# Batch 0's q and k in two parts of 256 and 320 tokens, four heads side by side

## The chip, the core and the metric

The kernel runs on one core of a Trainium2 chip. The core has a matrix engine (TensorE, "PE" in the profile, its weight loads "PEld"), a vector engine (VectorE, "DVE"), a scalar engine (ScalarE, "ACT"), GpSimd ("POOL"), which here mainly issues the loads, and SyncE ("SP"), which issues the stores. Each works through its own instructions in order and waits for the others by semaphores. The metric is the device time of one execution in microseconds (us); lower is better.

## What is computed

Eight batches of eight heads with 576 tokens of 64 elements. Heads 0 to 3 attend to the last 32 tokens, heads 4 to 7 to every fourth of the last 128. The attention's result, with the heads of a token side by side (4608 x 512), goes through two layers with a SiLU between them.

```python
scores = scale * np.matmul(q, k.transpose(0, 1, 3, 2))
rel = pos[:, None] - pos[None, :]
mask_plain = (rel >= 0) & (rel < window)                                   # window = 32
mask_dil = (rel >= 0) & (rel < window * dilation) & (rel % dilation == 0)  # dilation = 4
masks = np.stack([mask_plain if h < H // 2 else mask_dil for h in range(H)], axis=0)
scores = np.where(masks[None, :, :, :], scores, -1000000000.0)
attn = softmax over the last axis
x = np.matmul(attn, v), heads of a token side by side                      # 4608 x 512
h = x @ w_in                                                               # 512 x 2048
g = h * (1.0 / (1.0 + np.exp(-h)))
return (g @ w_out).astype(np.float32)                                      # 2048 x 512
```

## The kernel before

A batch goes through attention and then through the two layers. In the steady state the attention of later batches is spread by a hand-written plan (`plan_of`) between the products of the layers of an earlier one, so TensorE has products while the other engines do the softmax. Batch 0 has nothing to hide behind. It is written out by hand at the end of the kernel (lines 846 to 871), and it is cut into two parts of the sequence: part 0 is tokens 0 to 255, part 1 tokens 256 to 575. In the code z = 0 stands for the plain heads 0 to 3 and z = 1 for the dilated heads 4 to 7, `which` is 0 for q and 1 for k.

**Loads.** All loads are issued by GpSimd and change f32 to f16 on the way. Their order (lines 185 to 205) is: k and q of the dilated heads, the identity matrix, k and q of the plain heads (each a whole 576 tokens of four heads, `load_one`, line 108), two selections that build the band of the mask, v in eight loads, w_in in four quarters, batch 1's q and k, w_out in four quarters, batch 1's v. GpSimd uses eight semaphores in turn for them: a load is issued only when the eighth one before it has landed.

**Transposes.** Attention needs q and k with the 64 elements along the partitions. `transpose` (line 247) does that on TensorE, by products with the identity, into two PSUM tiles of pool `ps` (four buffers), and copies each tile to SBUF with one DVE copy and one ACT copy (`both`). The dilated heads land in `kC` and `qC`, sorted into the four classes of a token's number modulo 4; the plain ones in `kT` and `qT`. For batch 0 each of these four transposes takes the whole sequence, in the order k dilated, q dilated, k plain, q plain.

**Scores to values for batch 0.** `scores0(z, part)` (line 379) puts the mask into a PSUM tile of pool `big` (two buffers) by a product, adds the scores, and lets DVE take each row's maximum. `shift0` has DVE subtract it, after which ACT makes one exponential of the whole tile; or `scaled` scales the maximum and ACT makes one exponential for each of 8, 10 or 12 pieces, with its row sum (`exps`, line 499). `total` sums where ACT did not. `turn0` is DVE's normalisation and 32x32 transposition. `values0(z, part, idle)` (line 636) issues `idle` identity products of 256 columns and then the products with v; `finish0` casts the result to `xT`, by ACT for the dilated and DVE for the plain heads.

**Layer one for batch 0.** `layer1_part(f, part)` (line 683) multiplies w_in with part 0 or part 1 of `xT`; its first call issues three identity products more. Part 0 of all 2048 columns comes first, and into it are put `values0` of part 1 of the dilated heads (before the third group of four tiles) and of the plain heads (before the fourth). The SiLU of ACT writes `gT` (line 704), which layer two reads.

The order of each engine's instructions is the order of the calls. That of batch 0 is:

```python
    scores0(0, 0)
    scaled(0, 0)
    exps(0, 0, 0)
    turn0(1, 0)
    scores0(1, 1)
    scaled(1, 1)
    values0(1, 0, 3)
    finish0(1, 0, (act, act))
    exps(0, 1, 1)
    turn0(0, 0)
    scores0(0, 1)
    values0(0, 0, 2)
    finish0(0, 0)
```

Of the kernel before, what the change touches and what calls it, by code (L numbers as in the profile page):

```python
# [8 lines left out]
F16 = mybir.dt.float16  # L9
# [7 lines left out]
P = 128  # L17
W = 32
DIL = 4
# [4 lines left out]
HF = P // 2  # L24
URS = (9, 12)
DT = (3, 2)


@with_exitstack
def kernel(  # L30
# [9 lines left out]
    nc = tc.nc  # L40
# [51 lines left out]
    def tiles_qk(b):  # L92

        for which in (0, 1):
            t = nat.tile([P, GN[0] * QB + GN[1] * GW], F16, tag=f"n{which}", name=f"n{which}_{b}")
            sq = [
                t[:, 0 : GN[0] * QB].rearrange("p (g e) -> p g e", e=QB),
                t[:, GN[0] * QB :].rearrange("p (g e) -> p g e", e=GW),
            ]
            t = t[:, 0 : 2 * sum(URS) * D].rearrange("p (u d) -> p u d", d=D)  # L100
            u0, u1 = 2 * URS[0], 2 * (URS[0] + URS[1])
            qk[b, 0, which] = t[:, 0:u0].rearrange("p (h u) d -> p h u d", h=2)
            qk[b, 1, which] = t[0 : 2 * UPS[1] if b == 0 else P, u0:u1].rearrange("p (h u) d -> p h u d", h=2)
            for z in (0, 1):
                if b >= DT[z]:
                    qk[b, z, which] = sq[z]

    def load_one(b, z, which):

        src = (q, k)[which]  # L110
        if z == 0 or b == 0:
            nc.gpsimd.dma_start(  # L112
                out=qk[b, z, which].rearrange("p h u d -> p h (u d)"),
                in_=src[b, z * HH : z * HH + HH].rearrange("(h i) (p u) d -> (i p) h (u d)", i=2, u=URS[z]),
            )
            return
        for i in (0, 1):
            h = HH + 2 * i
            nc.gpsimd.dma_start(
                out=qk[b, z, which][i * HF : i * HF + UPS[z]].rearrange("p h u d -> p h (u d)"),  # L120
                in_=src[b, h : h + 2].rearrange("h (p u) d -> p h (u d)", u=URS[z]),
            )

    def load_squares(b, z, which):

# [50 lines left out]
    def load_w_out(c):  # L176
# [5 lines left out]

    band = cpool.tile([P, KB], F32, name="band")
    nc.vector.memset(band[0:W], 0.0)
    tiles_qk(0)
    load_one(0, 1, 1)
    load_one(0, 1, 0)
    make_identity(nc, ident)
    load_one(0, 0, 1)
    load_one(0, 0, 0)  # L190
    nc.gpsimd.affine_select(
        out=band[0:W], in_=band[0:W], compare_op=ALU.is_ge, fill=NEG,
        base=-1, pattern=[[1, KB]], channel_multiplier=-1,
# [2 lines left out]
        out=band[0:W], in_=band[0:W], compare_op=ALU.is_ge, fill=NEG,  # L196
        base=W, pattern=[[-1, KB]], channel_multiplier=1,
    )
    load_v(0)
    for c in range(4):  # L200
        load_w_in(c)
# [45 lines left out]
    def transpose(b, z, which, copies):  # L247

        a = att(b)
        src, n, ur = qk[b, z, which], UPS[z], URS[z]
        ts = [ps.tile([P, ur, n], F16, tag="ps", name=f"t{which}_{b}_{z}_{i}") for i in (0, 1)]
        if z and b == 0:
            for h in (0, 1):
                t = ts[h].rearrange("d (e i r) p -> d e i r p", i=2, r=2)
                for u in range(0, ur, 2):
                    nc.tensor.transpose(
                        t[:, u // DIL, :, u % DIL // 2, :],
                        src[:, h, u : u + 2, :].rearrange("p u d -> p (u d)"),  # L260
                        ident[0 : 2 * n, 0 : 2 * n],
                    )
        else:
            for u in range(0, ur, 1 + z):
                for h in (0, 1):
                    for i in (0, 1):
                        r = slice(i * HF, i * HF + n)
                        if z == 0:
                            o = (h + i) % 2 * D
                            dst, w = ts[h][o : o + D, u, :], src[r, h, u, :]  # L270
                        else:
                            dst = ts[i][:, u // DIL * 4 + 2 * h + u % DIL // 2, :]
                            w = src[r, h, u : u + 2, :].rearrange("p u d -> p (u d)")
                        nc.tensor.transpose(dst, w, ident[r, r])
        for i in (0, 1):
            if z == 0:
                o = (a["qT"][:, i], a["kT"][:, i, W:])[which]
                copies[i](o.rearrange("d (p u) -> d p u", u=ur), ts[i].rearrange("d u p -> d p u"))
            else:
                to_classes(a, which, i, ts[i].rearrange("d (e m) p -> d e m p", m=4), copies[i])  # L280

    def flat(b, z, which):

# [45 lines left out]
    def score(b, h, j, dst, start=True):  # L329

        if b >= DT[0]:
            score_turned(b, 0, h, 0, j, dst)
            return
        a = att(b)
        hp = h // 2
        o = (h + hp) % 2 * D
        r = slice(o, o + D)
        nc.tensor.matmul(
            dst[h * QB : h * QB + QB],
            a["qT"][r, hp, j * QB : j * QB + QB],  # L340
            keys(b, a["kT"][r, hp, j * QB : j * QB + KB]),
            start=start,
            stop=True,
            skip_group_check=not start,
        )
# [33 lines left out]
    def scores0(z, part):  # L379
# [20 lines left out]
        if z:  # L400
            for t in range(n):
                for e in (0, 1):
                    for h in range(HH):
                        for m in (0, 1):
                            score_class(0, h, 2 * e + m, 2 * part + t, sd[:, m, e * n + t], False)
        else:
            for j in range(w):
                for h in range(HH):
                    score(0, h, 8 * part + j, sd[:, j], False)
        nm = att(0)["nm", z, part] = stat.tile([P, WM], F32, tag="nm", name=f"nm_0_{z}_{part}")  # L410
        raw = sd[:, :, 0 : 2 * n] if z else sd[:, 0:w]
        d = nm[:, 0:w].rearrange("p (m t) -> p m t", m=2) if z else nm[:, 0:w]
        nc.vector.tensor_reduce(out=d, in_=raw, axis=AX.X, op=ALU.max, negate=True)
        a = att(0)
        a["raw", z, part] = raw

    def shift0(z, part):

# [264 lines left out]
    def layer1_part(f, part):  # L683
# [3 lines left out]
        n, w = ((4, SA), (2, 512))[part]  # L687
        if part == 0 and f == 0:
            hs = [ps.tile([P, 2, w], F32, tag="ps", name=f"h_0_{f}_{part}_{x}") for x in (0, 1)]
            warm(hs[0].rearrange("p n w -> p (n w)"), 3)  # L690
        else:
            hs = [big.tile([P, n, w], F32, tag="big", name=f"h_0_{f}_{part}")]
        m = n // len(hs)
# [148 lines left out]
    def turn0(z, part):  # L842
        normal(0, z, part)
        turned(0, z, part)

    transpose(0, 1, 1, both)
    build_mask_b()
    transpose(0, 1, 0, both)
    scores0(1, 0)
    shift0(1, 0)  # L850
    transpose(0, 0, 1, both)
    exps(0, 1, 0)
    transpose(0, 0, 0, both)
    total(0, 1, 0)
    scores0(0, 0)
    scaled(0, 0)
    exps(0, 0, 0)
    turn0(1, 0)
    scores0(1, 1)
    scaled(1, 1)  # L860
    values0(1, 0, 3)
    finish0(1, 0, (act, act))
    exps(0, 1, 1)
    turn0(0, 0)
    scores0(0, 1)
    values0(0, 0, 2)
    finish0(0, 0)
    shift0(0, 1)
    exps(0, 0, 1)
    turn0(1, 1)  # L870
# [51 lines left out]
```

## Time and profile before

| | |
|---|---|
| median of 3 runs | 307.88 us (306.43 to 309.94) |
| the profiled execution | 306.95 us, its span 305.1 us |
| busy: PE, PEld | 292.7 us (96% of the span), 186.9 us (61%) |
| busy: ACT, DVE, POOL | 206.4 us (68%), 199.7 us (65%), 119.6 us (39%) |
| layer-one products of batches 1 to 7 (L671) | 113.4 us |
| layer-two products of batches 1 to 7 (L740) | 113.8 us |
| DMA, read and written | 40.75 MB and 9.44 MB |

The profile is of one execution, by the hardware profiler; its span is the time from the first to the last instruction of the program, and the rest of the execution's time lies around it. A busy time is the sum of the stretches in which an engine worked at something. TensorE is the busiest engine, but products are pipelined and their ends are modelled, so its busy share is an upper one. A share over the whole span mixes the start, in which batch 0's attention has nothing beside it, with the long stretch after it.

### The profile page before, as it was taken

To read this page: it belongs to the slowest core of one execution; us is meant where nothing else is said; L and a number is where in the kernel's file an instruction comes from. 1 tells how busy PE (TensorE), PEld (TensorE's weight loads), DVE (VectorE), ACT (ScalarE), POOL (GpSimd) and SP (SyncE) were. 2 spreads that over 40 slices of the span, in tenths; PEclk is the share of its full clock that TensorE was granted. 3 is DMA by queue.
4 is the path that set the end of the run, shared out by engine and by line. 5 is a ranking of instruction groups with operands and counts; after the bars stand their busy time and mean duration, and the time that the engine had idled before them with its cause. 6 is when DMAs were issued, how large, how long until landed. Compare 5 with 4: busy or idle time off the path is not lost.

```text
span 305.1 us, 10290 instructions
## 1 busy us (share of the span) xinstructions
PE 292.7 (96%) x4400; PEld 186.9 (61%) x4400; DVE 199.7 (65%) x354; ACT 206.4 (68%) x688; POOL 119.6 (39%) x182
## 2 busy tenths in 40 slices
PE   2889999999999999999999999999999999999995
PEld 2458654577545774477645775477644775477544
DVE  2886589538898868966895768966895762820012
ACT  2497687865999559965894559975795559546200
POOL 8745347979964295336806086250000000000000
PEclk9999999999999999999999999999999999999999
DMA  6999999999994899499949199390002001110021
GB/s 109 158 205 206 208 157 170 189 185 126 118 184 87 89 70 128 119 106 41 126 71 184 37 62 134 106 118 4 3 34 105 37 2 36 54 52 0 19 86 69
DMA packets 111805, 30.47 MB, mean 100 GB/s; under 512 B 95520, under 2 KB 107280, under 8 KB 111760
## 3 DMA queue, kind: packets, MB, share of 16 engines
q0 software_dynamic: 106432, 20.38, 80.7%
q1 hardware_dynamic: 5328, 9.44, 8.5%
q8 instruction: 34, 0.56, 0.7%
q14 instruction: 11, 0.09, 0.1%
HBM read 40.75 MB, written 9.44 MB: 164 GB/s over the span
## 4 chain that ended last, share of the span: by engine, by line
PE 69%; DMA 16%; POOL 5%; DVE 4%; ACT 3%; issue 2%; POOLq 0%
PE h L671 32%; PE o L740 31%; DMA w_out<-in_moe_w_out_dram 5%; DMA n<-in_q_dram 5%; DMA w_in<-in_moe_w_in_dram 4%; PE x L588 3%; ACT pe L519 2%; DMA n<-in_k_dram 2%; PE s L327 2%; POOL n L132 2%; POOL n L112 1%; DMA vw<-in_v_dram 1%; DVE pn L541 1%; POOL w_in L171 1%; DVE ob L725 1%
## 5 line engine op out<-in xcount | busy, mean ns | idle before, releaser
L679 ACT ACTIVATE gT<-h 128x576 f16<-128x576 f32 x112 | 73.0, 651 | 60.5 <-PE h L671 60.4
L740 PE MATMUL o<-w_out,gT 128*128 128x512 f16 (+1 forms) x528 | 113.8, 373 | 0.0
L671 PE MATMUL h<-xT,w_in 128*128 128x288 f16 x896 | 113.4, 286 | 0.0
L671 PEld LDWEIGHTS <-w_in 128*128 128x128 f16 x896 | 86.6, 98 | 23.5 <-issue 0.2
L740 PEld LDWEIGHTS <-gT 128*128 128x128 f16 x528 | 50.7, 98 | 55.4
L519 ACT ACTIVATE pe<-ms,nm 128x64 f32<-128x64 f32 x238 | 78.9, 333 | 0.1
L725 DVE COPY ob<-o 128x512 f32<-128x512 f32 (+1 forms) x35 | 22.8, 664 | 45.4 <-PE o L740 44.1
L519 ACT ACTIVATION_READ_ACCUMULATOR pe<-ms,nm 128x1 f32 x238 | 44.5, 187 | 0.0
L132 POOL DMA_DIRECT2D n<-in_k_dram x44 | 31.9, 736 | 26.2 <-DVE kC L300 25.1
L372 DVE SCALAR_TENSOR_TENSOR ms<-s,mask 128x512 f32<-128x512 f32 x28 | 19.2, 686 | 28.6 <-PE s L327 19.9
L132 POOL DMA_DIRECT2D n<-in_q_dram x44 | 31.9, 735 | 3.5 <-DMA n<-in_q_dram 3.1
L154 POOL DMA_DIRECT2D vw<-in_v_dram x32 | 18.4, 580 | 34.4 <-PE x L588 31.8
L541 DVE TENSOR_TENSOR pn<-pe,r 128x640 f16<-128x640 f32 (+2 forms) x32 | 25.3, 792 | 1.1
L557 DVE STREAM_TRANSPOSE pt<-pn 128x640 f16<-128x640 f16 (+4 forms) x32 | 24.7, 772 | 1.1
L163 POOL DMA_DIRECT2D vw<-in_v_dram x32 | 21.1, 665 | 9.7 <-DMA w_out<-in_moe_w_out_dram 8.0
L439 DVE TENSOR_REDUCE nm<-ms 128x10 f32<-128x640 f32 (+1 forms) x28 | 22.0, 786 | 1.0
L696 PE MATMUL h<-xT,w_in 128*128 128x256 f16 (+1 forms) x128 | 18.6, 302 | 0.0
L588 PEld LDWEIGHTS <-vw 32*64 32x64 f16 (+1 forms) x1264 | 13.1, 107 | 7.4 <-issue 6.7
L588 PE MATMUL x<-pt,vw 32*64 32x64 f16 (+2 forms) x1264 | 15.0, 193 | 0.9 <-DVE pt L557 0.8
L696 PEld LDWEIGHTS <-w_in 128*128 128x128 f16 x128 | 12.7, 103 | 3.9 <-issue 0.2
L623 DVE CAST xT<-x 128x288 f16<-128x288 f32 x22 | 15.0, 819 | 0.0
L716 PE MATMUL o<-w_out,gT 128*128 128x512 f16 x64 | 14.7, 380 | 0.2 <-ACT ob L725 0.2
(84 smaller groups left out, 209.7 us busy)
## 6 DMA issues: line engine op xcount, KB each, us to landing
out_dram<-ob SPq DMA_DIRECT2D x35, 256.0 KB, 3.0
n<-in_k_dram POOLq DMA_DIRECT2D x24, 108.0 KB, 4.8
n<-in_q_dram POOLq DMA_DIRECT2D x24, 108.0 KB, 5.3
vw<-in_v_dram POOLq DMA_DIRECT2D x31, 80.0 KB, 3.7
vw<-in_v_dram POOLq DMA_DIRECT2D x32, 72.0 KB, 4.0
w_in<-in_moe_w_in_dram POOLq DMA_DIRECT2D x4, 512.0 KB, 9.3
w_out<-in_moe_w_out_dram POOLq DMA_DIRECT2D x4, 512.0 KB, 11.7
n<-in_k_dram POOLq DMA_DIRECT2D x20, 72.0 KB, 3.7
```

The source lines that it names most:

```text
L132: nc.gpsimd.dma_start(out=qk[b, z, which][o : o + QB], in_=bass.AP((q, k)[which].tensor, (b * H + z * HH + half * HH // 2) * S * D + x * Q ...
L163: nc.gpsimd.dma_start(out=vw[h * QB : h * QB + QB, 0:NB], in_=v[b, h].rearrange("(m p) d -> p m d", p=QB))
L439: nc.vector.tensor_reduce(out=nm[:, 0:w], in_=ms[:, 0:w], axis=AX.X, op=ALU.max, negate=True)
L519: nc.scalar.activation(pe[:, t, :], src[t], AF.Exp, bias=a["nm", z, hi][:, t : t + 1], scale=k, accum_out=l[:, t : t + 1],)
L541: nc.vector.tensor_tensor(pn[:, 0:w], a["pe", z, hi][:, 0:w], r[:, 0:w, None].broadcast_to([P, w, KB]), ALU.mult)
L557: nc.vector.transpose(out, src)
L588: nc.tensor.matmul(x[h // 2][h % 2 * D : h % 2 * D + D, col : col + wd], vws[b % 2][r, NB + kb * DIL + c if z else kb], turned_cols(b, pt[ ...
L671: nc.tensor.matmul(h[:, half, 0:HS], w_in16[:, c, f * P : f * P + P], xT[:, c, half * HS : half * HS + HS], start=(c == cs[0]), stop=(c == ...
L679: nc.scalar.activation(gT[:, f, s0 : s0 + S].rearrange("p (a c) -> p a c", a=2), h[:, :, 0:HS], AF.Silu)
L696: nc.tensor.matmul(hs[i // m][:, i % m, 0 : c1 - c0], w_in16[:, c, (f + i) * P : (f + i + 1) * P], xT[:, c, c0:c1], start=(c == 0), stop=( ...
L725: copy(ob, o)
L740: nc.tensor.matmul(o[:, 0, 0:m], gT[:, f, t * P : (t + 1) * P], w_out16[:, f, cols], start=(f == 0), stop=(f == NFF - 1),)
```

## The change

Batch 0's q and k no longer go through `nat` tiles and `transpose`. They are loaded in eight DMAs instead of four: part 0 (256 tokens) of k and q, dilated then plain, where the four whole loads stood, and part 1 (320 tokens) of all four behind the two selections and ahead of v. The four heads of a load lie one after the other along the partitions (4 x 32 rows of 8 tokens; part 1 is 4 x 16 rows of 20 tokens for the dilated heads, 4 x 32 rows of 10 for the plain ones), in space of `gT` that is written only later. `transpose0` replaces `transpose` for batch 0: one PSUM tile and one copy a part, by ACT for all but q of the dilated heads, which DVE copies. With four heads side by side a dilated transpose has 128 columns in part 0 (4 products) and 64 in part 1 (10 products); a plain part takes 16 and 20 products of 64x64.

The order of batch 0 changes with it. The transposes of part 1 stand behind `turn0(1, 0)`, and `scores0(1, 1)` behind `values0(1, 0)` and `finish0(1, 0)`; `values0(0, 0)` moves ahead of `scores0(0, 1)`. The maximum is a call of its own (`max0`), so DVE takes it in another place of its order; `total` moves behind `exps(0, 0, 0)`. Identity products: 2 and 1 ahead of the values instead of 3 and 2, and 1 ahead of layer one instead of 3, so four of eight. Plain heads lie in `qT` and `kT` by another rule (`score`), without a change in the count of score products.

```diff
+PU0 = (((32, 8), (32, 10)), ((32, 8), (16, 20)))
...
+    def rows0(z, which, part):
+        t = gT[:, 4 * z + 2 * which : 4 * z + 2 * which + 2, :].rearrange("p f c -> p (f c)")
+        pp, u = PU0[z][part]
+        o = part * PU0[z][0][1] * D
+        return t[0 : HH * pp, o : o + u * D].rearrange("p (u d) -> p u d", d=D)
+
+    def load_part(z, which, part):
+        pp, u = PU0[z][part]
+        nc.gpsimd.dma_start(
+            out=rows0(z, which, part).rearrange("p u d -> p (u d)"),
+            in_=bass.AP(
+                (q, k)[which].tensor, z * HH * S * D + part * SA * D, [[S * D, HH], [u * D, pp], [1, u * D]]
+            ),
+        )
...
-    tiles_qk(0)
-    load_one(0, 1, 1)
-    load_one(0, 1, 0)
+    load_part(1, 1, 0)
+    load_part(1, 0, 0)
     make_identity(nc, ident)
-    load_one(0, 0, 1)
-    load_one(0, 0, 0)
+    load_part(0, 1, 0)
+    load_part(0, 0, 0)
...
+    for z in (1, 0):
+        for which in (1, 0):
+            load_part(z, which, 1)
     load_v(0)
...
+    def transpose0(z, which, part, copy):
+        a = att(0)
+        pp, u = PU0[z][part]
+        src, t0 = rows0(z, which, part), part * SA
+        if z:
+            e = u // DIL
+            t = ps.tile([P, e, 2 * HH, pp], F16, tag="ps", name=f"t{which}_0_{z}_{part}")
+            for x in range(0, u, 2):
+                nc.tensor.transpose(
+                    t[:, x // DIL].rearrange("d (h r) p -> d r h p", r=2)[:, x % DIL // 2],
+                    src[:, x : x + 2, :].rearrange("p u d -> p (u d)"),
+                    ident[0 : HH * pp, 0 : HH * pp],
+                )
+            dst, o = ((a["qC"], 0), (a["kC"], W))[which]
+            o += t0 // DIL
+            copy(
+                dst[:, :, :, o : o + pp * e].rearrange("d h r (p e) -> d (h r) p e", e=e),
+                t.rearrange("d e m p -> d m p e"),
+            )
+        else:
+            t = ps.tile([P, u, 2 * pp], F16, tag="ps", name=f"t{which}_0_{z}_{part}")
+            for x in range(u):
+                for i in (0, 1):
+                    r = slice(i * HF, i * HF + HF)
+                    nc.tensor.transpose(t[r, x, :], src[r, x, :], ident[r, r])
+            dst = (a["qT"], a["kT"][:, :, W:])[which][:, :, t0 : t0 + pp * u]
+            copy(dst.rearrange("d h (p u) -> d h p u", u=u), t.rearrange("d u (h p) -> d h p u", h=2))
...
-            warm(hs[0].rearrange("p n w -> p (n w)"), 3)
+            warm(hs[0].rearrange("p n w -> p (n w)"), 1)
...
-    transpose(0, 1, 1, both)
+    transpose0(1, 1, 0, act)
     build_mask_b()
-    transpose(0, 1, 0, both)
+    transpose0(1, 0, 0, dve)
+    transpose0(0, 1, 0, act)
     scores0(1, 0)
+    max0(1, 0)
     shift0(1, 0)
-    transpose(0, 0, 1, both)
+    transpose0(0, 0, 0, act)
     exps(0, 1, 0)
-    transpose(0, 0, 0, both)
-    total(0, 1, 0)
     scores0(0, 0)
+    max0(0, 0)
     scaled(0, 0)
     exps(0, 0, 0)
+    total(0, 1, 0)
     turn0(1, 0)
+    transpose0(1, 1, 1, act)
+    transpose0(1, 0, 1, dve)
+    transpose0(0, 1, 1, act)
+    transpose0(0, 0, 1, act)
+    values0(1, 0, 2)
+    finish0(1, 0, (act, act))
     scores0(1, 1)
+    turn0(0, 0)
+    max0(1, 1)
     scaled(1, 1)
-    values0(1, 0, 3)
-    finish0(1, 0, (act, act))
     exps(0, 1, 1)
-    turn0(0, 0)
+    values0(0, 0, 1)
+    finish0(0, 0)
     scores0(0, 1)
-    values0(0, 0, 2)
-    finish0(0, 0)
+    max0(0, 1)
     shift0(0, 1)
```

More of the change, by code (lines that the diff above doesn't have):

```diff
@@ L102, in tiles_qk @@
             qk[b, 0, which] = t[:, 0:u0].rearrange("p (h u) d -> p h u d", h=2)
-            qk[b, 1, which] = t[0 : 2 * UPS[1] if b == 0 else P, u0:u1].rearrange("p (h u) d -> p h u d", h=2)
+            qk[b, 1, which] = t[:, u0:u1].rearrange("p (h u) d -> p h u d", h=2)
             for z in (0, 1):
@@ L110, in load_one @@
         src = (q, k)[which]
-        if z == 0 or b == 0:
+        if z == 0:
             nc.gpsimd.dma_start(
@@ L253, in transpose @@
         ts = [ps.tile([P, ur, n], F16, tag="ps", name=f"t{which}_{b}_{z}_{i}") for i in (0, 1)]
-        if z and b == 0:
+        for u in range(0, ur, 1 + z):
             for h in (0, 1):
[L256 to L274, printed above, removed]
+                for i in (0, 1):
+                    r = slice(i * HF, i * HF + n)
+                    if z == 0:
+                        o = (h + i) % 2 * D
+                        dst, w = ts[h][o : o + D, u, :], src[r, h, u, :]
+                    else:
+                        dst = ts[i][:, u // DIL * 4 + 2 * h + u % DIL // 2, :]
+                        w = src[r, h, u : u + 2, :].rearrange("p u d -> p (u d)")
+                    nc.tensor.transpose(dst, w, ident[r, r])
         for i in (0, 1):
@@ L280, in transpose @@
                 to_classes(a, which, i, ts[i].rearrange("d (e m) p -> d e m p", m=4), copies[i])
+    def transpose0(z, which, part, copy):
[17 more added lines that the diff above has]
+            )
+        else:
+            t = ps.tile([P, u, 2 * pp], F16, tag="ps", name=f"t{which}_0_{z}_{part}")
+            for x in range(u):
+                for i in (0, 1):
+                    r = slice(i * HF, i * HF + HF)
+                    nc.tensor.transpose(t[r, x, :], src[r, x, :], ident[r, r])
+            dst = (a["qT"], a["kT"][:, :, W:])[which][:, :, t0 : t0 + pp * u]
+            copy(dst.rearrange("d h (p u) -> d h p u", u=u), t.rearrange("d u (h p) -> d h p u", h=2))
     def flat(b, z, which):
@@ L334, in score @@
         a = att(b)
-        hp = h // 2
-        o = (h + hp) % 2 * D
+        hp, o = (h % 2, h // 2 * D) if b == 0 else (h // 2, (h + h // 2) % 2 * D)
         r = slice(o, o + D)
@@ L407, in scores0, with max0 @@
             for j in range(w):
-                for h in range(HH):
+                for h in (0, 2, 1, 3):
                     score(0, h, 8 * part + j, sd[:, j], False)
+        att(0)["raw", z, part] = sd[:, :, 0 : 2 * n] if z else sd[:, 0:w]
+    def max0(z, part):
+        w = width(0, z, part)
+        raw = att(0)["raw", z, part]
         nm = att(0)["nm", z, part] = stat.tile([P, WM], F32, tag="nm", name=f"nm_0_{z}_{part}")
-        raw = sd[:, :, 0 : 2 * n] if z else sd[:, 0:w]
         d = nm[:, 0:w].rearrange("p (m t) -> p m t", m=2) if z else nm[:, 0:w]
         nc.vector.tensor_reduce(out=d, in_=raw, axis=AX.X, op=ALU.max, negate=True)
-        a = att(0)
-        a["raw", z, part] = raw
     def shift0(z, part):
```

## The prediction

> **What bounds the kernel now.** I read the page's 40 slices first, then the timeline of all engines over the first 30 us, then single DMA issues with their time to landing, then the products of the first layer by half microseconds.
>
> ```profile
> PE   2889999999999999999999999999999999999995
> PEclk9999999999999999999999999999999999999999
> 120.00:160.00 40.00, 40.00 (x610) 24.87 (x609) 32.67 (x57) 32.73 (x138) 16.52 (x24) 1.00 0.99 92
> ```
>
> TensorE is busy from the fourth slice on; the third line (a stretch of 40 us, PE's busy time in its second field) has no gap at all. So the end is a start-up plus a fixed load of products. The change touches only the start-up, and is worth what it brings forward the point where PE stops waiting, at about 19.7 us, if nothing holds PE up again afterwards. The start-up in the timeline (start, length, engine, line; in brackets the idle time and what ended it):
>
> ```profile
> 5.61 1.14 PE L258 MATMUL t<-ident,n 96*128 96x96 f16 x12 [5.61 <-DMA n<-in_k_dram]
> 9.36 0.69 DVE L413 TENSOR_REDUCE nm<-s 128x8 f32<-128x512 f32 x1 [0.92 <-PE s L354]
> 10.84 0.70 PE L274 MATMUL t<-ident,n 64*64 64x64 f16 x36 [0.74 <-DMA n<-in_q_dram]
> 14.11 0.31 ACT L519 ACTIVATE pe<-s,nm 128x64 f32<-128x64 f32 x1 [1.86 <-DVE r L538]
> 16.45 1.33 ACT L657 CAST xT<-x 128x256 f16<-128x256 f32 x2
> 19.07 0.82 PE L631 MATMUL h<-ident 128*128 128x256 f16 x3
> 19.19 0.76 DVE L662 CAST xT<-x 128x256 f16<-128x256 f32 x2
> 19.69 5.19 PE L696 MATMUL h<-xT,w_in 128*128 128x256 f16 x32
> ...
> 25.43 1.92 PE L696 MATMUL h<-xT,w_in 128*128 128x256 f16 x16
> ```
>
> Four loads in a row (5.61, 6.98, 9.41, 10.84) pace it; the last, q of heads 0 to 3, releases the plain scores, and ACT's eight exponentials run from 14.11 to 16.45. From there ACT works without a pause. Layer one starts at 19.69, when DVE's first cast of xT is done (19.19 plus half of 0.76); the three identity products at 19.07 lie beside that cast. What stands behind it is w_in. POOL may have eight DMAs out, each issue waiting for the landing of the eighth before it, and these waits date the landings:
>
> ```profile
> 18.19 0.72 POOL L112 DMA_DIRECT2D n<-in_k_dram  x1 [1.21 <-DMA w_in<-in_moe_w_in_dram]
> 21.27 0.72 POOL L112 DMA_DIRECT2D n<-in_q_dram  x1 [2.35 <-DMA w_in<-in_moe_w_in_dram]
> 23.64 0.76 POOL L177 DMA_DIRECT2D w_out<-in_moe_w_out_dram  x1 [1.65 <-DMA w_in<-in_moe_w_in_dram]
> 26.51 2.31 POOL L177 DMA_DIRECT2D w_out<-in_moe_w_out_dram  x3 [2.12 <-DMA w_in<-in_moe_w_in_dram]
> ```
>
> About 0.28 us before each start a quarter of w_in had landed: 17.9, 21.0, 23.4, 26.2. PE asks for them at 19.69, near 22.6, at 25.43 and at 27.74: it is only 1.5 to 2 us behind the weights. That is the ceiling of any gain here.
>
> **The change, part by part.**
>
> *Loads.* Part 0 of one load is 4 x 256 x 64 x 2 B = 131 KB against 295 KB, 164 KB less. The stream runs at 207 GB/s (window 4 to 6 us), so each part 0 ahead saves 0.8 us. First k: 5.6 - 0.8 = 4.8; first q: 6.98 - 1.6 = 5.4. For the other two the issue comes to bind: POOL issues them near 3.2 and 3.9, and the quickest landing seen, 4.3 us after issue, less 0.8, gives 6.7 and 7.4 (before 9.37 and 10.80). The Trainium skill ("DMA: Bandwidth & Descriptors", Anatomy of one DMA) has about 2 us fixed per DMA plus bytes over 436 GB/s; by it 164 KB save 0.4 instead of 0.8 and the first q lands at 6.2, which changes nothing, as the third load gates PE.
>
> *First chain.* PE transposes that k (16 of 64x64, 0.45) to 7.1, then mask products and class scores; from their start to DVE's maximum took 1.30 (8.06 to 9.36), so the maximum is at 8.4 and the shift done 1.42 later (9.36 to 10.78), 9.8. The transposes of q0 stand behind the class scores on PE: 8.7; ACT's copy of 512 columns, 0.57 by its 0.64 for 576, 9.3; plain scores to maximum 0.74 (12.38 to 13.12), 10.1; maximum 0.69 and scaling 0.17, 11.0. The eight exponentials go 11.05 to 13.4 instead of 14.11 to 16.45: 3.0 us won. That is the whole of the benefit; what follows gives most of it back.
>
> *Second parts.* Four more loads, and 60 transposes that are now between turn0(1,0) and the values. Their landings (issued from 5.0 to 7.4, about 3.7 us each) are by 11 us and their PE time (about 2 us) lies under the exponentials. Their copies do not: k1's second copy waits on ACT behind the eight exponentials, 13.4 to 14.1 (0.71 for 640 columns), and the accumulators of values0 reuse its buffer, so PE stands until 14.1. From there PE is the chain itself, since class scores of part 1 have moved behind the values (before they ran at 12.99 under the exponentials): two identity products 0.53 (18.00 to 18.53), values 0.54 (18.53 to 19.07), mask and class scores 1.30 (12.99 to 14.29), one identity product 0.27, values 0.54, mask and plain scores 1.35 (16.64 to 17.99), one identity product 0.27: 4.80, so layer one starts at 18.9. The four identity products that go would cost 4 x 0.27 = 1.1 in this row; before, only the two ahead of the plain values were on the path. xT is ready: DVE's maximum of part 1 starts at 16.6, 1.1 with its scaling, casts 0.76, done 18.5.
>
> *Behind it.* ACT: two more copies to 15.5, casts of xT (1.0) to 16.5, then the twelve exponentials wait for that maximum until 17.7; before they began at 17.47. So they end 0.2 later, near 21.2. Its users: the transposed weights of class part 1 were ready at 23.24 and used at 24.81; they become 23.5 and 24.1. Those of plain part 1, ready at 26.03 and used at 27.28, become 26.3 and 26.5. The covers shrink to 0.6 and 0.2 but hold.
>
> *POOL and w_in.* Eight loads of 0.60 (the 48x2x768 form) to 0.73 (the old form) stand ahead of v instead of four: 4.8 to 5.8 against 2.9. Against that, the two waits of 0.81 and 0.77 inside the v loads fall, as the loads they waited for land earlier. w_in is issued 0.3 to 1.3 later than 11.73. Its landing has a queue in front (6.2 us for the first quarter), and the bytes ahead are the same, so its delay lies between -0.3 and +1.3; I take +0.3, nearer to the stream than to the issue: 18.2, 21.3, 23.7, 26.5. PE wants them at 18.9, 22.3, 24.7, 27.0.
>
> *Nothing else moves.* Transposes of batch 1 need loads that landed at 29.2 and ran at 30.68. The second-layer products start at 41.5 with w_out's first quarter in at 34.7. Batch 0's rows lie in gT, first overwritten by ACT behind products that need all of them.
>
> Sum: 19.69 - 18.9 = 0.8 won, 0.1 lost at the thin covers: 0.7. With the ends of w_in's delay it is 1.1 to 0.2.
>
> **The speed of PE.** The first 32 layer-one products took 5.19 us, the next 16 took 1.92.
>
> ```profile
> L696 PE MATMUL h<-xT,w_in x72: 272/273/421, 19.7 to 30.4; 128*128 128x256 f16 x64, 128*128 128x320 f16 x8
> 22.00:22.50 0.50, 0.50 (x4) 0.31 (x3) 1.00 1.28 221
> 23.00:23.50 0.50, 0.50 (x7) 0.46 (x5) 1.00 1.24 207
> ```
>
> Each takes 421 ns at first and 273 later, and the number under way per half microsecond goes from 4 to 7 near 22.6, while the granted clock stays at 1.00. All identity products before take 392 to 421: they are slow too, so taking four away cannot be seen to cost speed. I assume the step comes as long after the start of layer one as before.
>
> **Rivals.**
> (1) *The weights take the gain.* For: slack of 1.5 at the last quarter, one more DMA issue for each load. Against: equal bytes. At +1.3 the last quarter lands at 27.5 against a start at 27.74: gain 0.2, or a little below nothing, 307.2 to 307.7.
> (2) *PE stays slow longer: slower than before.* With fewer identity products and class scores and values in small pieces, the step comes after the first 32 products instead of near the 14th. A slow product costs about 0.10 more (0.21 against 0.11 spacing): 18 x 0.10 = 1.8, less the 0.7 won: 1.1 slower, 308.5. It decides from 7 further slow products on, that is a step later than 4.4 us after layer one starts. Against it: the identity products were never fast. The Trainium skill ("TensorE: Matmul & The Clock Gate", Part 1) says the clock doubles after a busy window of about 3.4 us, free-running, so that its point differs by run; the trace agrees as far as one step at 2.9 us goes, and by the rule less filler is a later step.
> (3) *PE is fast sooner*, since its work from 14.1 to 18.9 is without a pause. Then 14 slow products save 1.4, but the last quarter of w_in at 26.2 to 26.5 caps the gain at 1.5: 305.9.
> (4) *The change doesn't do what it says:* the third and fourth parts land no sooner than 9.4 and 10.8, because what follows mixes into the stream (k0 landed at 9.37 with v bytes already moved). Then the shift is done at 12.6, the exponentials run from 13.7 to 16.1, PE restarts at 16.8 and layer one starts at 21.6 by the same terms: 1.9 slower, 309.3. Against it: v is now issued behind all eight parts, and only 131 KB pieces stand ahead.
>
> **How the numbers follow.** The profiled execution took 306.95, 1.85 more than its span of 305.1; the sum gives 306.25 for it. The median of the three runs is 307.88, 0.9 above it; the middle of all four executions is 307.4, and minus 0.7 that is 306.7, my time. Chances: the forecast 0.50, rival 1 0.20, rival 2 0.11, rival 3 0.13, rival 4 0.06. Runs of one kernel lie between 306.43 and 309.94, so about 1% (3.1 us) is what a measurement tells from no change, and every case lies within it. The range adds some of this scatter: from 305.2 (rival 3 less 0.7) to 308.7, just over rival 2; rival 4 is left out. Faster by over 1% needs 304.8, below the ceiling set by w_in, by scatter alone: 0.09. Slower by over 1%, 311, needs rivals 2 and 4 together or scatter: 0.07. Within: 0.84.
>
> **What would show it.** Right: the first transposes at 4.8, ACT's first eight exponentials near 11, PE idle just before the values at 14.1, layer one near 18.9, w_in waits on POOL near 18.5, 21.6, 23.9, 26.8 or PE waiting for w_in by less than 0.5. Wrong: exponentials after 12, or layer one later than 19.7; a step of the product time from 421 to 273 elsewhere than 2.5 to 3.5 us after layer one starts; or a new PE wait between 24 and 31 us.

## The result, and the profile after

The change makes the kernel slower: 311.12 us (median of 6 runs, 310.68 to 312.37) against 307.94 (6 runs, 305.89 to 309.94), a ratio of 1.0116 with a 95% interval of 1.007 to 1.0163. The profiled execution took 311.06 us with a span of 308.9, 3.8 more than the span before. The prediction was 306.7, the other way.

The timeline of the changed kernel over the first 32 us, TensorE and ACT (start, length, engine, line, operation, count; in brackets the idle time ahead and what ended it):

```profile
6.92 0.61 PE L304 MATMUL t<-ident,gT 128*128 128x128 f16 x4 [6.92 <-DMA gT<-in_k_dram]
8.36 0.61 PE L304 MATMUL t<-ident,gT 128*128 128x128 f16 x4 [0.83 <-DMA gT<-in_q_dram]
10.15 0.64 PE L320 MATMUL t<-ident,gT 64*64 64x64 f16 x16 [1.19 <-DMA gT<-in_k_dram]
11.63 0.64 PE L320 MATMUL t<-ident,gT 64*64 64x64 f16 x16
...
14.85 0.31 ACT L563 ACTIVATE pe<-s,nm 128x64 f32<-128x64 f32 x1 [0.97 <-PE t L304]
...
17.18 0.73 ACT L311 COPY kC<-t 128x640 f16<-128x640 f16 x1
...
22.58 5.23 PE L740 MATMUL h<-xT,w_in 128*128 128x256 f16 x32
...
31.22 0.23 PE L632 MATMUL x<-pt,vw 32*64 32x64 f16 x5 [0.49 <-issue]
31.38 3.01 PE L740 MATMUL h<-xT,w_in 128*128 128x256 f16 x24
```

The four transposes stand where parts of 131 KB were to land at 4.8 to 7.4; they wait until 6.92, 8.36 and 10.15, later than the first whole load of 295 KB before (5.61). The eight exponentials start at 14.85 instead of 14.11, layer one at 22.58 instead of 19.69, and the last group of its first half at 31.38 instead of 27.74. From there TensorE is as busy as before (293.1 us against 292.7), so those 3.6 us reach the end.

POOL's issues in the same timeline date the rest:

```profile
10.39 0.57 POOL L173 DMA_DIRECT2D vw<-in_v_dram  x1 [1.21 <-DMA gT<-in_k_dram]
...
16.16 3.01 POOL L190 DMA_DIRECT2D w_in<-in_moe_w_in_dram  x4
...
22.82 0.72 POOL L113 DMA_DIRECT2D n<-in_k_dram  x1 [1.40 <-DMA w_in<-in_moe_w_in_dram]
25.34 0.70 POOL L113 DMA_DIRECT2D n<-in_q_dram  x1 [1.80 <-DMA w_in<-in_moe_w_in_dram]
27.88 0.77 POOL L196 DMA_DIRECT2D w_out<-in_moe_w_out_dram  x1 [1.84 <-DMA w_in<-in_moe_w_in_dram]
31.16 2.23 POOL L196 DMA_DIRECT2D w_out<-in_moe_w_out_dram  x3 [2.52 <-DMA w_in<-in_moe_w_in_dram]
```

Inside v's loads POOL now waits five times for slow parts (0.25, 1.21, 0.75, 0.71 and 0.45 us; one is shown), so w_in is issued at 16.16 instead of 11.73. By the same 0.28 us as in the prediction, its quarters land at 22.5, 25.1, 27.6 and 30.9 instead of 17.9, 21.0, 23.4 and 26.2. Two things are late at once: the attention, ready at 22.58, and the weights, at 22.5.

Why are small loads slower than large ones? The DMA view of the stretch from 2 to 6 us, packets and then one kind of issue (count, KB each, median us from issue to landing); before:

```profile
DMA packets 371, 0.55 MB, mean 136 GB/s; under 512 B 16, under 2 KB 371, under 8 KB 371
...
n<-in_k_dram POOLq DMA_DIRECT2D x2, 288.0 KB, 5.2
```

and after:

```profile
DMA packets 943, 0.16 MB, mean 39 GB/s; under 512 B 792, under 2 KB 943, under 8 KB 943
...
gT<-in_k_dram POOLq DMA_DIRECT2D x2, 128.0 KB, 6.2
```

More than twice the packets bring a third of the bytes, and 792 of 943 packets are under 512 B against 16. A load of 128 KB (the prediction's 131 KB, here in units of 1024 B) takes 6.2 us to land, one of 288 KB took 5.2. The page counts the whole execution:

```profile
DMA packets 114557, 30.48 MB, mean 99 GB/s; under 512 B 98272, under 2 KB 109904, under 8 KB 114512
```

Before it was 111805, so 2752 more, all of them under 512 B. Four more loads at 16 small packets each are 64 (e8 below has four loads more than before, and 64 packets more). The other 2688 are 12 x 224, and 224 is the number of rows of one head in the eight loads: 32 in six of them, 16 in the two dilated ones of part 1. This is the trail: a part load reads [4 heads][32 or 16 rows][row], and since a part of a head does not end where the next head begins, heads and rows cannot be merged into one dimension; the outermost size is 4. The explanation to be tested, theory A below, is that such a load is moved by 4 of the 16 DMA engines, while each of the other 12 gets a small packet for each row. The whole loads before had one merged dimension of 96 or 128 rows. The Trainium skill ("DMA: Bandwidth & Descriptors", "Why a DMA increments its semaphore by 16 and not by 1") states the selection: the number of engines is the largest one up to 16 that divides the slowest dimension of both sides. The packet counts here and below agree with it; it was not weighed in the prediction.

### The profile page after: what moved, and what is told of

Its sections match the earlier page's. It is cut to its first block, busy times and chain, and to the rows that moved or that the text cites. A ratio compares the mean times of both kernels' runs of the same rounds, so it can differ in the third digit from the quotient of the medians.

```text
span 308.9 us, 10303 instructions
## 1 busy us (share of the span) xinstructions
PE 293.1 (95%) x4400; PEld 187.3 (61%) x4400; DVE 198.7 (64%) x352; ACT 207.5 (67%) x690; POOL 122.3 (40%) x186
## 4 chain that ended last, share of the span: by engine, by line
PE 68%; DMA 17%; POOL 6%; DVE 4%; ACT 3%; issue 2%; POOLq 0%
PE h L715 32%; PE o L784 31%; DMA w_out<-in_moe_w_out_dram 4%; DMA w_in<-in_moe_w_in_dram 4%; PE x L632 3%; DMA gT<-in_q_dram 3%; DMA n<-in_k_dram 2%; DMA n<-in_q_dram 2%; ACT pe L563 2%; PE s L369 2%; POOL n L151 2%; DMA vw<-in_v_dram 1%; POOL gT L136 1%; POOL vw L182 1%; DVE pn L585 1%
## 5 line engine op out<-in xcount | busy, mean ns | idle before, releaser
L173 POOL DMA_DIRECT2D vw<-in_v_dram x32 | 18.4, 581 | 35.0 <-PE x L632 31.4
L740 PE MATMUL h<-xT,w_in 128*128 128x256 f16 (+1 forms) x128 | 18.6, 304 | 0.0
L740 PEld LDWEIGHTS <-w_in 128*128 128x128 f16 x128 | 12.7, 104 | 3.9 <-DMA w_in<-in_moe_w_in_dram 0.2
## 6 DMA issues: line engine op xcount, KB each, us to landing
w_out<-in_moe_w_out_dram POOLq DMA_DIRECT2D x4, 512.0 KB, 11.4
```

What stands on the lines that cost most here:

```text
L740: nc.tensor.matmul(hs[i // m][:, i % m, 0 : c1 - c0], w_in16[:, c, (f + i) * P : (f + i + 1) * P], xT[:, c, c0:c1], start=(c == 0), stop=( ...
```

## The experiments

**The pattern of the loads (e1).** All eight part loads read through one merged row dimension; sizes, places and order stay. Batch 0's q and k are then other tokens than the reference's.

```diff
-                (q, k)[which].tensor, z * HH * S * D + part * SA * D, [[S * D, HH], [u * D, pp], [1, u * D]]
+                (q, k)[which].tensor, z * HH * S * D + part * 8 * D, [[S // pp * D, HH * pp], [1, u * D]]
```

> The changed kernel, but the eight loads read the same number of rows of the same length at one common stride (128 rows of 8 tokens at a stride of 18 tokens; 128 of 10, or 64 of 20 at a stride of 36), so the source has one dimension of rows instead of 4 heads times 32 or 16. Batch 0 of the output is computed from other tokens than the reference's; the work is the same. Theory A (four engines: each part load is moved by 4 of the 16 DMA engines, because its outermost dimension is 4): first transposes near 5 us instead of 6.9, first eight exponentials near 11 to 11.5 instead of 14.85, layer one near 18.9 instead of 22.58, time 307 to 308, 2688 packets fewer (111869). Theory B (the new order, with copies behind the exponentials and class scores behind the values, is what costs): the loads may land sooner, but layer one stays later than 21 and the time over 309.5. Theory C (eight small loads cost a fixed time each, whatever their pattern): nothing moves, 311.

Measured: 307.5 us (10 runs, 306.55 to 309.63), ratio to before 1.0013 (0.9983 to 1.0043). The packets are 111869: the 2688 are gone, to the packet. Its timeline:

```profile
4.42 1.30 PE L304 MATMUL t<-ident,gT 128*128 128x128 f16 x8 [4.42 <-POOL band L209]
...
7.01 0.64 PE L320 MATMUL t<-ident,gT 64*64 64x64 f16 x16 [1.30 <-DMA gT<-in_k_dram]
...
11.76 0.31 ACT L563 ACTIVATE pe<-s,nm 128x64 f32<-128x64 f32 x1 [1.03 <-PE t L304]
...
19.04 0.39 PE L675 MATMUL h<-ident 128*128 128x256 f16 x1
19.62 5.02 PE L740 MATMUL h<-xT,w_in 128*128 128x256 f16 x32 [0.18 <-DMA w_in<-in_moe_w_in_dram]
```

The four-head pattern is the whole loss: without it the time is level with before. The exponentials start 2.35 sooner than before, but TensorE is ready for layer one only at 19.43 (19.04 and 0.39), 0.26 sooner than before: the rest of the lead goes, as the prediction said of its own 3.0, into the copies and scores that now stand between the exponentials and layer one. Most of the 0.26 then goes into a wait of 0.18 for w_in, and layer one starts at 19.62, near where it stood before (19.69). So two questions follow: does the number of engines carry this in the old kernel too, and why are the weights no earlier?

**Engines alone, on the kernel before (e2, e2c, e2b).** Its four loads of batch 0's q and k, the same bytes in the same order, with an outermost size of 4, of 8, or merged as a control (partly other tokens). The edit, for 4:

```diff
-        if z == 0 or b == 0:
+        if b == 0:
+            n, w = UPS[z] // 2, 2 * URS[z]
+            nc.gpsimd.dma_start(
+                out=qk[b, z, which].rearrange("p h u d -> p (h u d)"),
+                in_=bass.AP(src.tensor, z * HH * S * D, [[(n * w - 1) * D, 4], [w * D, n], [1, w * D]]),
+            )
+            return
+        if z == 0:
```

> The kernel before, whose four whole loads of batch 0 read rows of twice the length, in a source pattern of 4 blocks times 24 or 32 rows, the blocks' stride one token short of merging; nothing else is changed. Rows of batch 0 hold other tokens than the reference's. Theory A: each load runs on 4 DMA engines, some 6 us of data in each (24 rows of 3072 B at 0.25 us): first transposes near 9 instead of 5.6, the last load near 13 instead of 10.8, time 310 to 312, 1344 filler packets. Theories B and C: number and bytes of the loads are as before, so 307 to 308.5.

> The kernel before with its four loads of batch 0's q and k read as eight outer pieces that do not merge (a few other rows, so batch 0's q and k are not those of the reference). Theory A: the outermost size is the number of engines, so 8 engines move them, with fillers on the other 8: 8 x (12 + 12 + 16 + 16) = 448 packets more than 111357, that is 111805. First transposes between 5.9 (16 engines) and 12.4 (4 engines), near 7.5 to 9; time between 308.1 and 314.2, near 309.5 to 310.5. If it were the non-merging itself that costs (more descriptors, whatever the number of engines): first transposes near 12 and 314 again.

> Control for the run before it: the same long rows, 96 or 128 at one common stride, so nothing but the source's outermost dimension differs from it. Rows of batch 0 hold other tokens than the reference's. Theory A: 16 engines, 307 to 308.5, 448 packets fewer than the kernel before (111357). If it is as slow as the run before it, the row length and not the outermost dimension is what costs.

| outermost size | engines by theory A | small packets more | first transposes | layer one | time | ratio to before |
|---|---|---|---|---|---|---|
| merged | 16 | 0 | 5.91 | 19.80 | 308.07 | 1.0031 (0.9995 to 1.0067) |
| 8 | 8 | 448 | 6.93 | 22.03 | 310.04 | 1.0061 (1.0023 to 1.0099) |
| 4 | 4 | 1344 | 12.42 | 26.10 | 314.22 | 1.0222 (1.018 to 1.0264) |

The first transposes in the timelines, of 8 and then of 4:

```profile
6.93 1.14 PE L265 MATMUL t<-ident,n 96*128 96x96 f16 x12 [6.93 <-DMA n<-in_k_dram]
```

```profile
12.42 2.35 PE L265 MATMUL t<-ident,n 96*128 96x96 f16 x24 [12.42 <-DMA n<-in_k_dram]
```

Both packet counts are exact: 8 x 56 = 448 for eight, 12 x 112 = 1344 for four. The windows from 3 to 5 us, in the order of the table (the last field is GB/s):

```profile
3.00:5.00 2.00, 0.00 (x0) 0.00 (x0) 0.00 (x0) 0.00 (x0) 1.93 (x5) 1.00 0.89 157
3.00:5.00 2.00, 0.00 (x0) 0.00 (x0) 0.00 (x0) 0.00 (x0) 1.93 (x6) 1.00 0.42 75
3.00:5.00 2.00, 0.00 (x0) 0.00 (x0) 0.00 (x0) 0.00 (x0) 1.92 (x5) 1.00 0.43 42
```

The stream brings 157, 75 and 42 GB/s, near enough to 16, 8 and 4 parts of 16. The packet records of the three traces say why: a data packet of 3072 B takes 0.25 us (median) in each, but on average 15.4, 8.5 and 5.0 of them are under way at once in that stretch. The small packets hold 4 bytes and take 7 ns each, so they are a mark and not the cost. The change shows the same against e1: 5.1 data packets under way against 14.8, each 0.10 us in both. So it is the number of engines, and not that the dimensions fail to merge: 8 also does not merge, and costs about a third as much; against the merged control its time alone would not tell (the intervals overlap), its landings do. Against the expectations, 8 came earlier than 7.5 to 9, and 4 later than near 9: 12.42, and there 24 transposes run without a pause, so q had landed nearly as soon as k. Whole loads on four engines cost even more than the parts of the change do (1.0222 against 1.0116).

**Identity products (e3).** The changed kernel with all eight instead of four of them.

```diff
-            warm(hs[0].rearrange("p n w -> p (n w)"), 1)
+            warm(hs[0].rearrange("p n w -> p (n w)"), 3)
...
-    values0(1, 0, 2)
+    values0(1, 0, 3)
...
-    values0(0, 0, 1)
+    values0(0, 0, 2)
```

> The changed kernel with its four identity products put back (3, 2 and 3 again). Theory D (PE's product time steps down later for want of identity products): the step from 421 to 273 ns comes at least 1 us sooner after layer one's start, time 309 to 310. Theory A: PE is the chain from the values on, so four more cost up to 4 x 0.27 = 1.1 us: 311 to 312.3.

Measured: 311.34 us (310.36 to 311.92), ratio 1.0131 (1.0087 to 1.0175): no better than the change. The timeline shows why it cannot be:

```profile
23.60 2.02 PE L740 MATMUL h<-xT,w_in 128*128 128x256 f16 x16
26.26 0.94 PE L740 MATMUL h<-xT,w_in 128*128 128x256 f16 x7 [0.64 <-DMA w_in<-in_moe_w_in_dram]
```

Layer one starts 1.0 later, its products are fast almost at once (16 in 2.02; the step that theory D speaks of comes about 0.5 us after layer one starts), and TensorE then waits 0.64 for the second quarter of w_in. So theory D's step came and its 309 to 310 did not: the removed identity products are not the loss. That they moved the step is not shown by one execution, as it moves between executions of the other kernels too (see below).

**Which loads (e5a, e5b).** Only part 0, or only part 1, merged as in e1.

```diff
-                (q, k)[which].tensor, z * HH * S * D + part * SA * D, [[S * D, HH], [u * D, pp], [1, u * D]]
+                (q, k)[which].tensor, z * HH * S * D + part * (8 * D if part == 0 else SA * D),
+                [[S // pp * D, HH * pp], [1, u * D]] if part == 0 else [[S * D, HH], [u * D, pp], [1, u * D]],
```

> The changed kernel with only the four loads of part 0 read through one merged row dimension (other tokens of batch 0, so its q and k are not those of the reference); part 1 keeps the four-head pattern. Theory A (a load with four heads outermost is moved by 4 of 16 DMA engines): part 0 lands as in the fully merged version (first transposes 4.4, eight exponentials from 11.8 to 12.5) and 4 x 12 x 16 or 32 fillers of part 1 stay: 115 or so rows of 12, that is 112 x 12 = 1344 packets more than 111869. The lateness of the weights is the other half: w_in is issued only when part 1 has landed, between 13.3 and 16.2, layer one between 20 and 22, time 308.5 to 310. If only the late part 0 counts (theory A1): 307.5. If only the late weights count (theory A2): 311.

> The reverse: only the four loads of part 1 are read through one merged row dimension (other tokens of batch 0), part 0 keeps the four-head pattern. Theory A: first transposes near 6.9 and the eight exponentials from 14.5 to 14.9 as in the changed kernel, layer one 22 to 22.6 from that alone; 4 x 12 x 32 = 1536 packets more than 111869; w_in issued between 13.3 and 16.2. Time 309.5 to 311. If only the late part 0 counts (A1): 311. If only the late weights count (A2): 307.5 to 308.5.

Part 0 merged: 312.86 us, ratio 1.0183 (1.012 to 1.0247), no faster than the change. Part 1 merged: 310.85, 1.0122 (1.006 to 1.0184), as slow as the change. The packets are 1152 and 1536 more than in e1 (12 x 96 and 12 x 128; the 112 rows in the first expectation were miscounted). No theory had e5a above the change. Its timeline:

```profile
11.33 0.31 ACT L564 ACTIVATE pe<-s,nm 128x64 f32<-128x64 f32 x1 [0.80 <-DVE nm L479]
...
24.25 5.44 PE L741 MATMUL h<-xT,w_in 128*128 128x256 f16 x32 [2.14 <-DMA w_in<-in_moe_w_in_dram]
```

Its exponentials come 3.5 sooner than in the change, and layer one 1.7 later. The slow loads of part 1 act twice. They hold TensorE, whose transposes of part 1 wait for a load until 16.26, so that it is ready at 22.1, only 0.5 sooner than in the change. And they hold POOL, one wait alone 3.74, so w_in is issued at 17.15 and TensorE waits 2.14 for it. In e5b TensorE is ready at 21.9 and w_in, issued at 15.21, lands at 21.9 too; layer one starts at 21.95. So early exponentials alone bring nothing here: part 1 and the weights have to land as well.

**The same tokens on 16 engines (e7).** Rows outermost and heads inside, the order undone by a permuted identity; plain parts in two loads of two heads, so twelve loads.

```diff
+        n = HH if z else 2
+        for h in range(0, HH, n):
...
-                (q, k)[which].tensor, z * HH * S * D + part * SA * D, [[S * D, HH], [u * D, pp], [1, u * D]]
+                    (q, k)[which].tensor, (z * HH + h) * S * D + part * SA * D,
+                    [[u * D, pp], [S * D, n], [1, u * D]],
```

> The change with the same tokens, but with the rows outermost and the heads inside in every part load (32 or 16 rows, then heads), the order of the heads undone by a permuted identity in the transposes; the plain parts are two loads of two heads each, so there are twelve loads instead of eight. It computes the reference. Theory A: all 16 engines work at each load and no filler is left: packets within some 100 of 111869. First transposes 4.4 to 5, eight exponentials from 11.8 to 13, w_in issued 13.3 to 15.5 (four issues more on POOL, about 0.6 each), layer one 19.6 to 21, time 307.5 to 309. If the pattern of four heads is not the cause, 310.5 to 311.5 as the changed kernel.

> The rows-outermost version once more, beside the next one on the same chip; its first profiled execution, 312.2, stood at the long end of its own runs (307.5 to 313.0), with the first quarter of w_in landed at 21.9 and TensorE waiting 2.7 for it. If the landing of w_in is what sets this kernel's time (rival 1), a shorter execution shows the same eight exponentials at 11 and a smaller wait ahead of layer one, and the execution's time follows the landing: 309 to 310 goes with a wait of 0 to 1. If the time varies for another reason, the wait is again near 2.7.

Measured: 309.82 us, 1.0052 (1.0019 to 1.0084); again 309.45, 1.0054 (1.0019 to 1.0089). Slower than before, faster than the change. The second look:

```profile
10.86 0.31 ACT L567 ACTIVATE pe<-s,nm 128x64 f32<-128x64 f32 x1 [0.80 <-DVE nm L482]
...
18.59 0.39 PE L679 MATMUL h<-ident 128*128 128x256 f16 x1
20.63 6.38 PE L744 MATMUL h<-xT,w_in 128*128 128x256 f16 x32 [1.65 <-DMA w_in<-in_moe_w_in_dram]
```

Here is the prediction's chain: exponentials at 10.86 (predicted 11.05), TensorE ready at 19.0 (predicted 18.9). But w_in lands at 20.6, and the 32 products behind the wait take 6.38 instead of 5.19. The first profiled execution, 312.24 us, had a wait of 2.74 and 6.60 for the products; the second, 309.35 us, 1.65 and 6.38. Of the 2.9 us between the two, 1.5 are there at the last group of part 0 (31.41 against 29.88) and go with the landing; the other 1.4 is a single wait of TensorE for DVE's transposed weights at 93.7, which has nothing to do with it. The second wait is also larger than the 0 to 1 expected. That a pause makes the products slower is not shown: in e5a they took 5.44 behind a wait of 2.14, and without a wait 3.96 (e8) to 5.80 (e5b).

Why is w_in late with 16 engines at work and no byte more? Mostly because it is issued late: at 13.28 in e1 and 13.89 in e7_again against 11.73, and from there to its landing it takes 6.3 and 6.7 us against 6.2 (6.4 in the change, issued at 16.16). POOL needs 0.5 to 0.7 us to issue a piece of 64 to 160 KB, with the identity and the two selections in between, and in e1 it also waits 1.23 for a load of part 1. The stream carries less, too. Windows of 2 to 18 us (the last two fields are the DMA engines' busy share and GB/s); before, e1 and e7_again:

```profile
2.00:18.00 16.00, 10.06 (x292) 6.44 (x292) 9.79 (x22) 7.08 (x28) 13.24 (x24) 1.00 1.26 162
```

```profile
2.00:18.00 16.00, 10.71 (x286) 7.08 (x287) 9.05 (x21) 7.85 (x26) 14.36 (x27) 1.00 1.19 142
```

```profile
2.00:18.00 16.00, 11.43 (x296) 7.48 (x299) 9.26 (x22) 8.24 (x28) 15.73 (x30) 1.00 1.13 135
```

By 18 us 2.59 MB have moved before (162 x 16), 2.27 in e1, 2.16 in e7 and 1.84 in the change (115). Part of this only follows from the late issue; but from 6 to 8 us, long before w_in, e7_again moves 104 GB/s at a DMA share of 0.84, where before moved 172 at 1.15. That the smaller pieces leave the stream short there is a reading of these rows; the next two runs test it.

**Two tests of that (e8, e9).** e8 is the kernel before with each of the four loads cut in two halves of the rows; e9 is e7 with the first quarter of w_in issued between v's dilated and plain loads. Both leave the result as it is.

```diff
-        if z == 0 or b == 0:
+        if b == 0:
+            n = UPS[z]
+            for i in (0, 1):
+                nc.gpsimd.dma_start(
+                    out=qk[b, z, which][i * n : i * n + n].rearrange("p h u d -> p h (u d)"),
+                    in_=src[b, z * HH : z * HH + HH].rearrange("(h i) (p u) d -> i p h (u d)", i=2, u=URS[z])[i],
+                )
+            return
```

```diff
+        if b == 0:
+            load_w_in(0)
         for h in range(HH):
```

> The kernel before with each of its four loads of batch 0's q and k as two loads of half the rows (16 engines each, the same bytes, the same order otherwise); it computes the reference. Theory S: eight smaller issues fill the stream more slowly at the start, so fewer bytes have moved by 18 us than the 2.59 MB of before, w_in is issued 1 to 2.5 later than 11.73 and its first quarter lands 0.5 to 1.7 later than 17.9, at 18.4 to 19.6, still ahead of layer one; first transposes 5.6 to 6.2; time 307.7 to 308.7. If the number of loads costs nothing beyond the issue: w_in lands at 17.9 to 18.2, no difference.

> The rows-outermost version with the first quarter of w_in issued between v's four loads for the dilated heads and v's four for the plain heads. Theory S (the DMA stream is the bound: everything ahead of layer one has to come through it): the quarter lands 2 to 3 sooner than in e7_again, but the plain v lands as much later, the values of the plain heads (near 16.8 in the rows-outermost version) wait for it, and layer one starts no sooner than within 0.5 of e7_again; time within 1 of it. Theory R (only w_in's place in POOL's order is late): layer one starts near 19.5 without a wait, the time is 307 to 308.

e8: 307.71 us, 0.9999 (0.9972 to 1.0027). w_in is issued at 12.39 and lands at 18.35, 0.45 later, with 2.48 MB moved by 18 us, still ahead of layer one, so it costs nothing. That is more than no loss and less than theory S expected (issue after 12.7, landing 18.4 to 19.6). With as many loads as e1 and the same bytes it loses 0.11 MB where e1 loses 0.32, so the number of loads by itself explains only a part of e1's late weights; what makes the rest, beyond e1's wait of 1.23 on POOL, is not shown. e9: 312.92 us, 1.0187 (1.0126 to 1.0249), 3.5 above e7:

```profile
19.86 0.25 PE L638 MATMUL x<-pt,vw 32*64 32x64 f16 x1 [2.82 <-DMA vw<-in_v_dram]
21.62 0.47 PE L638 MATMUL x<-pt,vw 32*64 32x64 f16 x2 [1.50 <-DMA vw<-in_v_dram]
```

Theory R is wrong: the quarter lands only 1.3 sooner (19.25), the plain values wait 4.5 us for v, and layer one starts at 24.36. Theory S is right that the order cannot be gained from, but the price was worse than its "within 1".

**Less ahead of w_in (e10, e11).** e7 and before, each without the loads of four of batch 0's eight heads of v (zeros in their place).

```diff
+    nc.vector.memset(vws[0][HF:P], 0.0)
...
-        for h in range(HH):
+        hv = HH if b else 2
+        for h in range(hv):
```

> The rows-outermost version (e7) without the loads of four of batch 0's eight heads of v (zeros in their place, so batch 0's output is not the reference's): four issues and 0.3 MB less ahead of w_in, so that w_in is issued near 11.3 instead of 13.9 and its first quarter lands near 18. Theory W (the weights take the gain; the prediction's chain holds otherwise): the wait of 1.65 ahead of layer one is gone, layer one starts at 18.6 to 19.0, as predicted for the change, the last group of four tiles starts at 26.5 to 27.7, and the time is 0.7 to 2 below e11, 305.5 to 307. If another cost than w_in stands in the way (theory P, slow products or ACT): layer one near 19 but the time within 0.5 of e11.

> Control: the kernel before without the same loads of v. Its w_in lands some 2 sooner too, but TensorE is at the first quarter only at 19.7, as in before: theory W says that it gains nothing, ratio 0.997 to 1.003. If the stream held before back as well, it is faster by 1 or more.

e11: 308.35 us, 1.0005 (0.998 to 1.003): before gains nothing from lighter loads, though its first quarter now lands at 16.4. e10: 307.5 us, 0.999 (0.9971 to 1.0008): e7 gains 1.9 (309.45 to 307.5). The difference of the two means is 0.67 with an uncertainty of 0.63 (12 runs each), on the side of theory W at its lower edge; against before, neither is told from no change. Theory W's 305.5 to 307 was missed, and so was its layer one at 18.6 to 19.0: w_in, issued at 11.21, landed at 19.4 and not near 18.

```profile
19.44 5.09 PE L746 MATMUL h<-xT,w_in 128*128 128x256 f16 x32 [0.34 <-DMA w_in<-in_moe_w_in_dram]
```

So even this version waits for the weights. From issue to landing the first quarter needs 8.2 us here, 8.2 in e9 and 8.7 in e11, the three where it is issued soonest, against 6.2 before: an earlier issue is only in part an earlier landing. Why it needs that long with less ahead of it stays open.

## Why the prediction was wrong

*The step that failed* is "Loads": "164 KB less ... so each part 0 ahead saves 0.8 us". It sized a load by its bytes alone and took the stream's 207 GB/s for granted. The first loads landed 2.1 to 4.0 later than predicted (6.92, 8.36, 10.15 and 11.4, by POOL's wait, against 4.8, 5.4, 6.7 and 7.4). The diff held the cause, three dimensions in place of a mergeable two, and the prediction read past it. Where 16 engines work (e1, e7) the step's sizes hold to within 0.7 us: first transposes at 4.42 and 4.49 (predicted 4.8), exponentials at 11.76 and 10.86 (predicted 11.05).

*POOL and w_in* was mis-sized, on the assumption that equal bytes ahead mean an equal landing. Predicted +0.3 (at most +1.3); measured +4.6 in the change, +1.7 in e1, +2.7 in e7. It took the delay to lie "nearer to the stream than to the issue"; the issue came 4.4, 1.6 and 2.2 later, so it lay at the issue and a little above it. "The two waits inside the v loads fall" became five waits with 3.4 us together. The ceiling that the prediction named, TensorE 1.5 to 2 us behind the weights, was the right row; the change lowers that ceiling.

*Second parts and the chain of TensorE* had the right length, 5.5 predicted and 5.4 measured from the end of the exponentials to layer one (17.18 to 22.58), but in part by luck, as TensorE is released by another copy than predicted:

```profile
17.69 0.58 PE L675 MATMUL x<-ident 128*128 128x256 f16 x2 [1.68 <-DVE qC L311]
```

It is DVE's copy of q, done at 17.64, and not ACT's copy of k behind the exponentials, which goes on to 17.91. In e1, e3, e5b, e7 and e9, too, TensorE starts about 0.05 after DVE's copy. The 4.8 from there to layer one were 4.9. Four identity products less did no harm to the time (e3).

*The thin cover* of the last values of part 1 (predicted 0.2 left) did not show as a late softmax; 0.49 of idle time stands there (31.22), put down to "issue". It is most of the 0.7 that comes on top between the start of layer one (2.9 late) and its last group (3.6 late). A like pause shows in e1 (0.54), e2c (0.57), e3 (1.15) and e11 (0.22) and is missing in e5a and e7. It is most likely TensorE waiting for its own instructions. In all five traces with the pause it ends 1.4 to 1.6 us after a 16 KB transfer of the DMA queue "instruction" (in the change that transfer ends at 29.60, the pause at 31.22). It stands at the same product in four of them, and four products sooner in e3, which has four identity products more in front. In before, e5a and e7 that transfer was over at least 1.5 us ahead of this product. No run tests this, and the prediction has no term for it.

*The speed of PE* was right for the change: the number of products under way per half microsecond goes from 5 to 7 near 25.8, 3.2 after layer one starts, against 2.9 before. Rival 2 (slow for longer) is not what happened here. The step does move by more than a microsecond between executions: the first 32 products took 3.96 to 6.60 over the runs.

*The rivals.* Rival 4, "parts land no sooner", at a chance of 0.06, is what came about, with layer one at 21.6 predicted and 22.58 measured, but its mechanism (other loads mixing in) is not the one found. Its argument against, "only 131 KB pieces stand ahead", is the error itself. Rival 1, the weights take the gain, is what remains once the pattern is mended: of the 0.8 predicted, 0.7 is there in e7 when TensorE is ready (18.98 against 19.69), and w_in takes it and 0.9 more; in e1 only 0.26 was left to take. e10 and e11 lean the same way, at the edge of their noise. No version run here is faster than before by more than its interval; e1 and e8 are level with it.

## What to carry to other kernels

Before giving a smaller load a smaller price, write its access pattern as the DMA gets it: if the cut stops two dimensions from merging, look at the size of the outermost one that is left, and at whether the small-packet count grows by (16 less that size) for each row. Where a start-up has both a chain and a stream of loads, price the change for both: here 2.4 to 3.3 us won at the exponentials (e1, e7) were 0.3 to 0.7 when TensorE was ready for layer one, and worth nothing, as the weights came last. Each further load also takes time of the engine that issues it (0.5 to 0.7 us here), and what stands behind is issued later, so equal bytes ahead do not mean an equal landing.

## What the runs showed of the hardware

The packet counts of loads with an outermost size of 4 or 8 come out exactly as one small packet for each row on every engine that moves none of the load: 2688, 1344, 1536, 1152 and 448. From 3 to 5 us the rate was about proportional to that size (157, 75 and 42 GB/s for 16, 8 and 4), with packets as quick in each; the first landings were not, as the first transposes stood at 5.91, 6.93 and 12.42; in e2 the second load had landed by then as well. And with nearly the same work ahead, the first 32 products of layer one took 5.19 us in before and 4.16 in e2b, while the granted clock in the profile's rows stayed at 1.00 in both.
